# The last output block in two column halves, and new ranks in a list planner (gated linear recurrence followed by a SiLU MLP)

## The chip, the cores and the metric

One core of a Trainium2 chip. Times are device microseconds of one execution; the metric is the median of several runs. A profile is one execution, recorded by the hardware profiler; its span runs from the first to the last instruction.

## The reference

A recurrence with a forget gate over 768 positions, for 4 batches and 8 heads of 48 channels, and then an MLP with SiLU over the 3072 rows that come out of it:

```python
f = 1 / (1 + exp(-f_logit))                      # q, k, v, f_logit: [4, 8, 768, 48]
for t in range(768):
    state = f[:, :, t, :, None] * state + einsum('bhd,bhe->bhde', k[:, :, t], v[:, :, t])
    y[:, :, t] = einsum('bhd,bhde->bhe', q[:, :, t], state)
x = y.transpose(0, 2, 1, 3).reshape(3072, 384)   # heads side by side
h = x @ w_in                                     # w_in: [384, 2048]
out = (h * (1 / (1 + exp(-h)))) @ w_out          # w_out: [2048, 384]
```

## The kernel before

The work is cut into 12 blocks m, each with two units j. A unit is 128 positions of one batch, all heads: a block holds 256 rows of x. Block m belongs to chunk m // 2 of the sequence, so units of block m need the state that block m - 2 left (`st`).

A unit's recurrence is done in chunk form. `logs` takes ln(1 + exp(-f)) on ScalarE (task L), `cumsum` sums it along positions on TensorE (cs), `inverse` and `forward` take exponentials of it (ia, aa), `scale_k` on GpSimd and `scale_q` on VectorE multiply k and q by them (ki, qg). TensorE transposes both (T), VectorE copies the result out (qk), TensorE makes the scores (A), VectorE masks them (am), TensorE makes the outputs from scores and state (Y), VectorE copies them (yc), TensorE turns them so that channels stand on partitions (X), and VectorE copies that into `xT`. `update` (D) and `state` (st) carry the state on. Block 0 is laid out in another way (WIDE), which the change does not touch.

The MLP of a block: `mlp_in` (tasks I) makes h transposed, with w_in as weights, in 8 groups of six matmuls that stream 256 columns (both units) into one PSUM tile `h_ps`, and `silu` (S) writes it to `hT` in bf16. For blocks listed in SPLIT, `mlp_in_unit` and `silu_unit` do one unit at a time: twelve matmuls of 128 columns a group, again 8 groups a block. `mlp_out` (O) multiplies hT of a unit by w_out into `o_ps`, in four groups of four matmuls of 384 columns; `result` (R) copies it on ScalarE to `o_sb`, and `store` (G) sends 128 rows of 384 floats to the output, from GpSimd's queue for blocks under 8 and from SyncE's (SP) from block 8 (LATE) on. `h_ps`, `o_ps` and the fillers share three PSUM buffers.

The weights come in eight DMAs from GpSimd (`load_w_in` and `load_w_out`, 512 columns or 4 row tiles each), which are held back until ki of block 1, unit 1 has been done (BEFORE). The inputs come through SP's queue, into eight rotating buffers for each of f, k, q and v.

The order of everything is made at build time by the class `Plan`. Each task has an engine, a cost in us written in the code, the tasks that it needs, the buffers that it takes and frees, and a rank. `Plan.run` walks through time: of the tasks that could start first on an engine it takes the one with the lowest rank. The ranks are base = 8m + 3j (W["m"], W["j"]) plus an offset for each kind (W), and 1000 and more for the MLP, which so fills what the recurrence leaves. A TensorE task of block 3 or later is planned to start at least `spare` after the producer on another engine is done, over and above a fixed allowance (DRAIN). `patience` says how long the planner stays in one of the modes "MLP in" and "MLP out" on TensorE, since ScalarE has to load a table (`act_table`) when it turns from exponentials to SiLU. Where TensorE would wait for more than `slack`, the planner puts in filler matmuls on zeros (`warm`). The instructions are then written out in the order of the planned starts; each engine executes its own in that order, and waits by semaphores. So the planned times set the order and nothing else.

The groups of the views, by line: 489 narrow MLP-in matmuls, 504 wide ones, 519 MLP out, 524 the copy of the result, 530 its store, 535 fillers, 330 qg, 327 ki, 386 scores, 441 turns, 497 and 513 SiLU.

Of the kernel before, what the change touches and what calls it, by code (L numbers as in the profile page):

```python
# [11 lines left out]
F32 = mybir.dt.float32  # L12
# [6 lines left out]
class Plan:  # L19
# [58 lines left out]
    def run(self, filler=None):  # L78
# [5 lines left out]
        holder = {}  # L84
        left = dict(tasks)
        for t in tasks.values():
            for n in t["needs"]:
                assert n in tasks, (t["name"], n)
        self.silus = self.ins = self.exps = turned = 0
        while left:  # L90
            best = None
            fronts = {}
            for t in left.values():
                ready = 0.0
                for n in t["needs"]:
                    if n not in end:
                        ready = None
                        break
                    ready = max(ready, end[n] + (self.DRAIN.get(tasks[n]["engine"], 0.1) + t["spare"]) * (tasks[n]["engine"] != t["engine"]))
                if ready is None:  # L100
                    continue
# [24 lines left out]
            if e in ("LD", "WT"):  # L126
# [5 lines left out]
                if t["emit"] is not None:  # L132
                    self.order.append((start, t["emit"]))
                del left[t["name"]]
                continue
# [32 lines left out]
            self.log.append((start, end[t["name"]], e, t["name"]))  # L168
            del left[t["name"]]
        self.span = max(end.values())  # L170
# [17 lines left out]

    patience = 0.7
    slack = 0.4  # L190
    spare = 0.8

# [6 lines left out]
def kernel(  # L199
# [10 lines left out]
    nc = tc.nc  # L210
# [303 lines left out]

    def mlp_out(m, j, n):
        if n == 0:
            os[m, j] = hps.tile([C, d_model], F32, name="o_ps", tag="h_ps")
        for i in range(n, n + 4):
            nc.tensor.matmul(os[m, j], hT[m][:, i, j * C:(j + 1) * C], w_out_sb[:, i, :],  # L519
                             start=(i == 0), stop=(i == NT - 1))  # L520

    def result(m, j):
        osb[m, j] = wk.tile([C, d_model], F32, name="o_sb", bufs=4)
        nc.scalar.copy(osb[m, j], os[m, j])  # L524

    def store(m, j):
# [38 lines left out]
    for m in range(NH):  # L565
# [56 lines left out]
        for j in range(HB):  # L622
            for n in range(0, NT, 4):
                add(f"O{m}.{j}.{n}", "PE", 0.655, do(mlp_out, m, j, n),
                    [f"S{m}.{j}.{n}" if m in SPLIT else f"S{m}.{n + 2}", f"wo{n}"] + ([f"O{m}.{j}.{n - 4}"] if n else []),
                    rank=1000 + m * 10 + 5 + j + n * 0.1, takes="h" if n == 0 else None,
                    frees=[owner] if n == NT - 4 and j == HB - 1 else None)
            add(f"R{m}.{j}", "ACT", 0.5, do(result, m, j), [f"O{m}.{j}.{NT - 4}"], rank=-500.0, frees=[f"O{m}.{j}.0"])
            add(f"G{m}.{j}", *(("SP", 0.05) if m >= LATE else ("POOL", 0.85)), do(store, m, j), [f"R{m}.{j}"], rank=-501.0)
            add(f"W{m}.{j}", "DMA", 0.6, None, [f"G{m}.{j}"], rank=-1)  # L630

# [70 lines left out]
```

## Time and profile before

| | |
|---|---|
| runs, us | 195.43, 194.62, 194.53, 196.70, 195.81; median 195.43 |
| the profiled execution | 195.43 us, its span 193.7 us |
| granted TensorE clock | 1.00 |
| busy: TensorE, weight loads, VectorE, ScalarE, GpSimd | 96%, 73%, 58%, 67%, 29% |
| matmuls: MLP out, MLP in wide, MLP in narrow, fillers | 384, 432, 288, 75 of 2127 |
| table loads on ScalarE | 14, 1283 ns each |

The page counts a matmul from its issue to the end of its way through the array, so that matmuls overlap: what a group costs TensorE is the distance of starts and not the mean duration. In the lines shown further on, an entry such as "PE h_ps L504 x6" is TensorE, the tile written, the line and the number of matmuls; in the chain the two numbers ahead of it are start and length in us. A bracket at the end of a timeline row is the idle time of the engine ahead of it and what ended it. PEld is TensorE's weight load. In a row of groups, the part after the last bar is the idle time ahead of the group and what released it.

### The profile page before, as it was taken

What the parts mean: (1) busy time and instruction counts of PE and PEld (TensorE: products, weight loads), DVE (VectorE), ACT (ScalarE), POOL (GpSimd) and SP (SyncE); (2) the same over time, 40 slices, a digit from 0 to 9 for tenths busy, and PEclk for the clock granted to TensorE, in tenths of its full rate; (3) what the DMA queues carried; (4) which work ended last, traced back from release to release, by engine and by line L of the source; (5) the groups of instructions that cost most, each with busy time, mean ns of one, the idle gap of its engine ahead of it and who ended that gap; (6) DMA issues with size and microseconds to landing.
All of it is one profiled execution on the core that took longest, in us unless ns stands there. A gap on an engine that the chain in (4) does not pass through costs nothing.

```text
span 193.7 us, 5153 instructions
## 1 busy us (share of the span) xinstructions
PE 185.9 (96%) x2127; PEld 141.0 (73%) x2127; DVE 113.0 (58%) x222; ACT 130.5 (67%) x244; POOL 56.9 (29%) x84
## 2 busy tenths in 40 slices
PE   7789988999999999999999999999999999999993
PEld 3457767999666687878688688976688679886661
DVE  6188866652059993877379989726887883000000
ACT  2754556768876569898989995799775027993111
POOL 7343990010375423341571332007820000000000
PEclk9999999999999999999999999999999999999999
DMA  5999999998999999999999996001120020000222
GB/s 126 220 213 174 190 194 190 185 186 168 214 240 252 213 218 196 229 219 211 223 238 216 181 238 148 3 0 41 44 81 3 0 85 0 0 3 0 81 81 81
DMA packets 101654, 27.06 MB, mean 140 GB/s; under 512 B 96256, under 2 KB 100864, under 8 KB 101632
## 3 DMA queue, kind: packets, MB, share of 16 engines
q1 hardware_dynamic: 94784, 19.67, 52.0%
q0 software_dynamic: 4736, 6.29, 14.4%
q10 hardware_dynamic: 2112, 0.79, 2.2%
q8 instruction: 16, 0.26, 0.5%
q14 instruction: 6, 0.05, 0.1%
HBM read 25.17 MB, written 4.72 MB: 154 GB/s over the span
## 4 chain that ended last, share of the span: by engine, by line
PE 80%; DMA 9%; DVE 3%; POOL 3%; issue 2%; ACT 1%; ACTq 0%; DVEq 0%; POOLq 0%
PE o_ps L519 31%; PE h_ps L504 23%; PE h_ps L489 8%; DMA w_in_sb<-in_moe_w_in_dram 6%; PE t_ps L363 5%; DMA q_w<-in_q_dram 3%; PE a_ps L386 3%; PE y_ps L420 2%; PE y_ps L416 2%; PE x_ps L441 2%; PE cs L314 2%; PE d_ps L460 1%; DVE qg L330 1%; POOL ki L327 1%; PE al_ps L351 1%
## 5 line engine op out<-in xcount | busy, mean ns | idle before, releaser
L519 PE MATMUL o_ps<-w_out_sb,hT 128*128 128x384 bf16 x384 | 68.6, 326 | 0.0
L504 PE MATMUL h_ps<-xT,w_in_sb 128*128 128x256 bf16 x432 | 52.1, 273 | 0.9 <-DMA w_in_sb<-in_moe_w_in_dram 0.9
L519 PEld LDWEIGHTS <-hT 128*128 128x128 bf16 x384 | 36.2, 98 | 21.3
L513 ACT ACTIVATE hT<-h_ps 128x512 bf16<-128x512 f32 x72 | 42.4, 597 | 12.3 <-PE h_ps L504 9.8
L504 PEld LDWEIGHTS <-w_in_sb 128*128 128x128 bf16 x432 | 40.5, 98 | 6.4 <-DMA w_in_sb<-in_moe_w_in_dram 1.4
L327 POOL TENSOR_TENSOR ki<-k_ld,ia 128x384 bf16<-128x384 f32 x22 | 22.3, 1018 | 29.6 <-ACT ia L319 22.5
L330 DVE TENSOR_TENSOR qg<-q_ld,a 128x384 bf16<-128x384 f32 x22 | 19.8, 905 | 19.2 <-ACT a L324 19.0
L397 DVE TENSOR_TENSOR atm<-a_ps,triu 128x512 bf16<-128x512 f32 x44 | 28.3, 686 | 3.9 <-PE a_ps L386 3.8
L524 ACT COPY o_sb<-o_ps 128x384 f32<-128x384 f32 x24 | 11.5, 478 | 26.2 <-PE o_ps L519 26.0
L336 POOL CAST vb<-v_ld 128x384 bf16<-128x384 f32 x22 | 12.5, 567 | 40.1 <-DMA v_ld<-in_v_dram 34.9
L368 DVE COPY qk<-t_ps 128x1024 bf16<-128x1024 bf16 x24 | 16.4, 685 | 4.8 <-PE t_ps L363 4.7
L287 ACT ACT_TABLE_LOAD x14 | 18.0, 1283 | 1.8 <-PEq L686 1.6
L489 PE MATMUL h_ps<-xT,w_in_sb 128*128 128x128 bf16 x288 | 18.5, 219 | 0.0
L435 DVE CAST y<-y_ps 128x384 bf16<-128x384 f32 x22 | 12.2, 554 | 10.0 <-PE y_ps L420 9.9
L489 PEld LDWEIGHTS <-w_in_sb 128*128 128x128 bf16 x288 | 16.6, 98 | 0.6
L535 PE MATMUL w_ps<-zeros 128*128 128x384 bf16 x75 | 15.6, 351 | 1.2 <-DVE zeros L643 1.2
L497 ACT ACTIVATE hT<-h_ps 128x512 bf16<-128x512 f32 x24 | 13.9, 597 | 3.9 <-PE h_ps L489 3.1
L319 ACT ACTIVATE ia<-cs 128x384 f32<-128x384 f32 x24 | 11.4, 485 | 4.8 <-PE cs L314 4.1
L530 POOL DMA_DIRECT2D out_dram<-o_sb x16 | 9.3, 584 | 11.6 <-ACT o_sb L524 7.5
L301 ACT ACTIVATE f_ld<-f_ld 128x384 f32<-128x384 f32 x22 | 11.6, 526 | 1.5 <-DMA f_ld<-in_f_logit_dram 1.4
L480 DVE TENSOR_TENSOR states<-sd,al 48x192 bf16<-48x192 f32 x32 | 11.8, 368 | 0.8
L302 ACT ACTIVATE lf<-f_ld 128x384 bf16<-128x384 f32 x22 | 11.5, 523 | 0.7
(76 smaller groups left out, 198.3 us busy)
## 6 DMA issues: line engine op xcount, KB each, us to landing
f_ld<-in_f_logit_dram SPq DMA_DIRECT2D x22, 192.0 KB, 4.1
k_ld<-in_k_dram SPq DMA_DIRECT2D x22, 192.0 KB, 4.3
q_ld<-in_q_dram SPq DMA_DIRECT2D x22, 192.0 KB, 4.2
v_ld<-in_v_dram SPq DMA_DIRECT2D x22, 192.0 KB, 4.1
out_dram<-o_sb POOLq DMA_DIRECT2D x16, 192.0 KB, 3.5
w_in_sb<-in_moe_w_in_dram POOLq DMA_DIRECT2D x4, 384.0 KB, 9.6
w_out_sb<-in_moe_w_out_dram POOLq DMA_DIRECT2D x4, 384.0 KB, 17.5
out_dram<-o_sb SPq DMA_DIRECT2D x8, 192.0 KB, 1.9
```

The lines of the kernel that those rows point to most:

```text
L287: nc.scalar.preload_act_table_set(tables[name])
L327: nc.gpsimd.tensor_mul(slots(m, ki[m % 4][:, j, :, 0:D]), flip(m, loaded[m, j, "k"]), slots(m, ias[m, j]))
L330: nc.vector.tensor_mul(slots(m, qg[m % 4][:, j, :, 0:D]), flip(m, loaded[m, j, "q"]), slots(m, aas[m, j]))
L336: nc.gpsimd.tensor_copy(vb[m % 4][:, j], loaded[m, j, "v"])
L368: nc.vector.tensor_copy(qkT[m, j], t_ps[m, j])
L397: nc.vector.tensor_mul(atm[m, j][:, r], att[m, j][:, r], triu[:, None, :].to_broadcast([C, NP, C]))
L489: nc.tensor.matmul(h_ps[:, i], w_in_sb[:, kk, (n + i) * 128:(n + i + 1) * 128], xT[m][:, kk, j], start=(kk == 0), stop=(kk == KT - 1))
L497: nc.scalar.activation(hT[m][:, n:n + 4, j * C:(j + 1) * C], hs[m, j, n], AF.Silu)
L504: nc.tensor.matmul(h_ps[:, i], w_in_sb[:, kk, (n + i) * 128:(n + i + 1) * 128], xT[m][:, kk].rearrange("p b c -> p (b c)"), start=(kk == 0 ...
L513: nc.scalar.activation(hT[m][:, n:n + 2, :], hs[m, n], AF.Silu)
L519: nc.tensor.matmul(os[m, j], hT[m][:, i, j * C:(j + 1) * C], w_out_sb[:, i, :], start=(i == 0), stop=(i == NT - 1))
L535: nc.tensor.matmul(w_ps[:, 0:NP * 2 * D], zeros[:, 0:128], zeros, start=True, stop=True)
```

## The change

Three things, in one diff.

The last unit's MLP-out (block 11, unit 1) is made in two column halves of 192, each with its own PSUM tile, its own four groups, its own copy and its own store; the second half's groups come after the first's. All other units keep 384 columns.

The numbers that the planner goes by are other ones: all ranks in W except that of m, SPLIT (blocks 1, 2, 3 before, 2 alone after), `patience` (0.7 to 0.5), `spare` (0.8 to 0.5), and the block from which `spare` holds (3 to 5). The cost of a result's copy is 0.05 higher.

The planner's bookkeeping: it keeps a list of the tasks whose needs are done, with their ready times, and breaks ties of rank by the order in which tasks were added, as they stood in its table before.

```diff
-        spare = self.spare if engine == "PE" and m >= 3 else 0.0
+        spare = self.spare if engine == "PE" and m >= self.spare_from else 0.0
...
-            for t in left.values():
-                ready = 0.0
-                for n in t["needs"]:
...
+            for t in could.values():
+                if t["name"] not in ready_at:
+                    ready_at[t["name"]] = max([0.0] + [
...
-                choice = min(now, key=lambda c: c[2]["rank"])
+                choice = min(now, key=lambda c: (c[2]["rank"], place[c[2]["name"]]))
...
-    patience = 0.7
+    patience = 0.5
     slack = 0.4
-    spare = 0.8
+    spare = 0.5
+    spare_from = 5
...
-    def mlp_out(m, j, n):
+    def mlp_out(m, j, n, cols):
         if n == 0:
-            os[m, j] = hps.tile([C, d_model], F32, name="o_ps", tag="h_ps")
+            os[m, j, cols] = hps.tile([C, d_model], F32, name="o_ps", tag="h_ps")
+        lo, hi = cols
         for i in range(n, n + 4):
-            nc.tensor.matmul(os[m, j], hT[m][:, i, j * C:(j + 1) * C], w_out_sb[:, i, :],
+            nc.tensor.matmul(os[m, j, cols][:, lo:hi], hT[m][:, i, j * C:(j + 1) * C], w_out_sb[:, i, lo:hi],
                              start=(i == 0), stop=(i == NT - 1))
...
-    def result(m, j):
-        osb[m, j] = wk.tile([C, d_model], F32, name="o_sb", bufs=4)
-        nc.scalar.copy(osb[m, j], os[m, j])
+    def result(m, j, cols):
+        lo, hi = cols
+        osb[m, j, cols] = wk.tile([C, d_model], F32, name="o_sb", bufs=4)
+        nc.scalar.copy(osb[m, j, cols][:, lo:hi], os[m, j, cols][:, lo:hi])
...
-        eng.dma_start(out=out[r0:r0 + C, :], in_=osb[m, j])
+        eng.dma_start(out=out[r0:r0 + C, lo:hi], in_=osb[m, j, cols][:, lo:hi])
...
-    W = dict(m=8, j=3, L=0, cs=0, ia=-15, aa=1, ki=4, qg=1, vb=-8, T=7, qk=1, A=7, am=-2, Y=11,
-             yc=1, D=25, st=-3, X=4, xT=-9, al=-4, ea=3, va=13)
+    W = dict(m=8, j=6, L=-8, cs=1, ia=-11, aa=-5, ki=1, qg=3, vb=-13, T=28, qk=10, A=3, am=10, Y=15,
+             yc=6, D=12, st=-4, X=-27, xT=-18, al=-28, ea=-4, va=36)
     LATE = 8
-    SPLIT = (1, 2, 3)
+    SPLIT = (2,)
...
+            parts = [(0, d_model)] if (m, j) != (NH - 1, HB - 1) else [(0, d_model // 2), (d_model // 2, d_model)]
+            for part, cols in enumerate(parts):
+                part = "abc"[part]
+                share = (cols[1] - cols[0]) / d_model
+                for n in range(0, NT, 4):
+                    add(f"O{m}.{j}.{n}{part}", "PE", 0.655 * share, do(mlp_out, m, j, n, cols),
...
+                        rank=1000 + m * 10 + 5 + j + n * 0.1 + 2 * (part == "b"), takes="h" if n == 0 else None,
...
+                add(f"R{m}.{j}{part}", "ACT", 0.5 * share + 0.05, do(result, m, j, cols), [f"O{m}.{j}.{NT - 4}{part}"],
+                    rank=-500.0, frees=[f"O{m}.{j}.0{part}"])
+                add(f"G{m}.{j}{part}", *(("SP", 0.05) if m >= LATE else ("POOL", 0.85)), do(store, m, j, cols),
+                    [f"R{m}.{j}{part}"], rank=-501.0)
```

More of the change, by code (lines that the diff above doesn't have):

```diff
@@ L85, in run, with done @@
         left = dict(tasks)
+        place, users, missing, ready_at = {}, {}, {}, {}
         for t in tasks.values():
-            for n in t["needs"]:
+            place[t["name"]] = len(place)
+            missing[t["name"]] = len(set(t["needs"]))
+            for n in set(t["needs"]):
                 assert n in tasks, (t["name"], n)
+                users.setdefault(n, []).append(t["name"])
+        could = {n: t for n, t in tasks.items() if not missing[n]}
+        def done(name):
+            for u in users.get(name, ()):
+                missing[u] -= 1
+                if not missing[u]:
+                    could[u] = tasks[u]
+            del left[name], could[name]
         self.silus = self.ins = self.exps = turned = 0
@@ L92, in run @@
             fronts = {}
-            for t in left.values():
-                ready = 0.0
[L95 to L101, printed above, removed]
+            for t in could.values():
+                if t["name"] not in ready_at:
+                    ready_at[t["name"]] = max([0.0] + [
+                        end[n] + (self.DRAIN.get(tasks[n]["engine"], 0.1) + t["spare"]) * (tasks[n]["engine"] != t["engine"])
+                        for n in t["needs"]])
+                ready = ready_at[t["name"]]
                 p = self.pool_ready(t, end)
@@ L133, in run @@
                     self.order.append((start, t["emit"]))
-                del left[t["name"]]
+                done(t["name"])
                 continue
@@ L168, in run @@
             self.log.append((start, end[t["name"]], e, t["name"]))
-            del left[t["name"]]
+            done(t["name"])
         self.span = max(end.values())
@@ L513, in silu, with store @@
         nc.scalar.activation(hT[m][:, n:n + 2, :], hs[m, n], AF.Silu)
-    def mlp_out(m, j, n):
+    def mlp_out(m, j, n, cols):
         if n == 0:
-            os[m, j] = hps.tile([C, d_model], F32, name="o_ps", tag="h_ps")
+            os[m, j, cols] = hps.tile([C, d_model], F32, name="o_ps", tag="h_ps")
+        lo, hi = cols
         for i in range(n, n + 4):
-            nc.tensor.matmul(os[m, j], hT[m][:, i, j * C:(j + 1) * C], w_out_sb[:, i, :],
+            nc.tensor.matmul(os[m, j, cols][:, lo:hi], hT[m][:, i, j * C:(j + 1) * C], w_out_sb[:, i, lo:hi],
                              start=(i == 0), stop=(i == NT - 1))
-    def result(m, j):
-        osb[m, j] = wk.tile([C, d_model], F32, name="o_sb", bufs=4)
-        nc.scalar.copy(osb[m, j], os[m, j])
-    def store(m, j):
+    def result(m, j, cols):
+        lo, hi = cols
+        osb[m, j, cols] = wk.tile([C, d_model], F32, name="o_sb", bufs=4)
+        nc.scalar.copy(osb[m, j, cols][:, lo:hi], os[m, j, cols][:, lo:hi])
+    def store(m, j, cols):
+        lo, hi = cols
         g, b = m // 2, m % 2 * HB + j
@@ L622 @@
         for j in range(HB):
[L623 to L630, printed above, removed]
+            parts = [(0, d_model)] if (m, j) != (NH - 1, HB - 1) else [(0, d_model // 2), (d_model // 2, d_model)]
[4 more added lines that the diff above has]
+                    add(f"O{m}.{j}.{n}{part}", "PE", 0.655 * share, do(mlp_out, m, j, n, cols),
+                        [f"S{m}.{j}.{n}" if m in SPLIT else f"S{m}.{n + 2}", f"wo{n}"]
+                        + ([f"O{m}.{j}.{n - 4}{part}"] if n else []),
+                        rank=1000 + m * 10 + 5 + j + n * 0.1 + 2 * (part == "b"), takes="h" if n == 0 else None,
+                        frees=[owner] if n == NT - 4 and j == HB - 1 and cols == parts[-1] else None)
+                add(f"R{m}.{j}{part}", "ACT", 0.5 * share + 0.05, do(result, m, j, cols), [f"O{m}.{j}.{NT - 4}{part}"],
+                    rank=-500.0, frees=[f"O{m}.{j}.0{part}"])
+                add(f"G{m}.{j}{part}", *(("SP", 0.05) if m >= LATE else ("POOL", 0.85)), do(store, m, j, cols),
+                    [f"R{m}.{j}{part}"], rank=-501.0)
+                add(f"W{m}.{j}{part}", "DMA", 0.6 * share, None, [f"G{m}.{j}{part}"], rank=-1)
     pieces = [("wi", load_w_in, n) for n in range(0, d_ff, 512)] + [("wo", load_w_out, n) for n in range(0, NT, 4)]
```

## The prediction

> **What bounds the kernel now.** I read the busy shares first, then the slices, then the chain that ended last, then TensorE's own pieces of it, and last the end of the span. The first view gives shares only:
>
> ```profile
> PE 185.9 (96%) x2127; PEld 141.0 (73%) x2127; DVE 113.0 (58%) x222; ACT 130.5 (67%) x244; POOL 56.9 (29%) x84
> ...
> PE   7789988999999999999999999999999999999993
> ...
> DMA  5999999998999999999999996001120020000222
> ...
> PE 80%; DMA 9%; DVE 3%; POOL 3%; issue 2%; ACT 1%; ACTq 0%; DVEq 0%; POOLq 0%
> ```
>
> The slices say more than the share: from about the sixth to the last PE stands at 9, so the time is the sum of PE's work from its first MLP group to its last, plus the few holes in it, plus the tail. The reader is to see that a moved instruction on DVE, ACT or POOL is worth nothing unless PE waits for it.
>
> The holes show in the timeline of PE about 33 us and in the chain about 62 to 67 us. The columns are start and duration in us.
>
> ```profile
> 31.72 0.83 PE L489 MATMUL h_ps<-xT,w_in_sb 128*128 128x128 bf16 x12
> 33.05 0.83 PE L504 MATMUL h_ps<-xT,w_in_sb 128*128 128x256 bf16 x6 [0.50 <-DMA w_in_sb<-in_moe_w_in_dram]
> ```
> ```profile
> 62.13 1.39 DVE qg L330
> 63.52 0.48 DVE sd L477
> ...
> 64.75 0.56 DVE y L435
> ...
> 65.34 1.30 DVE atm L397 x2
> ...
> 66.68 0.40 PE a_ps L386 x8
> ```
>
> The first pair: twelve narrow matmuls take 0.67 us, so PE was free at 32.39 and stood 0.66 us for a piece of w_in. The second: DVE is the chain for 4.5 us (62.13 to 66.64); PE had ended its transposes x_ps (start 66.16, 0.17 long) at 66.33, a score group starts about 0.10 late after any other kind of group (62.07 after an o_ps group that began at 61.32 and issues for 0.65), so 0.25 us of the 0.35 is a true wait. I find no third hole over 0.1 us after 27 us, except one filler matmul w_ps at 75.9 (0.16 us), which is a hole that the plan filled. So after 27.0 us PE has only 0.66 + 0.25 + 0.16 = 1.07 us that isn't work.
>
> The unit costs of PE, and the end:
>
> ```profile
> 34.42 0.66 PE h_ps L504 x6
> ...
> 35.25 0.67 PE h_ps L489 x12
> ```
> ```profile
> L524 ACT COPY o_sb<-o_ps 128x384 f32<-128x384 f32 x24 | 11.5, 478 | 26.2 <-PE o_ps L519 26.0
> ...
> out_dram<-o_sb SPq DMA_DIRECT2D x8, 192.0 KB, 1.9
> ```
> ```profile
> 190.45 0.48 ACT L524 COPY o_sb<-o_ps 128x384 f32<-128x384 f32 x1 [1.47 <-PE o_ps L519]
> ```
>
> The last matmul ends at 190.37, the copy runs to 190.93, the store is issued at 190.96 and lands 1.9 us later, and the closing semaphores bring the span to 193.7. The tail after PE is 3.3 us.
>
> **What the Trainium skill says.** "TensorE: Matmul & The Clock Gate", section "Back-to-back issue gap", gives N/2.4 + 2.5 ns for one matmul of N columns, and a slower 81 ns for N=128 where a weight load goes with each. The trace agrees with the first (0.67/12 = 56 ns at 128, 0.655/6 = 109 ns at 256, 0.65/4 = 163 ns at 384) and not with the 81. "ScalarE: Activation LUTs", section "What ACT_TABLE_LOAD costs", has a fixed part of 186 ns and 0.833 ns per column, and 1283 ns for a table load; the trace has 478 ns for 384 columns, somewhat under, and 1283 ns for the load. "DMA: Bandwidth & Descriptors", section "Latency and other measured facts", puts the fixed cost of a transfer near 2 us, mostly the round trip; the 1.9 us of these stores agrees, so half the bytes cannot halve it. "GPSIMD Engine Reference", section "1. Specifications", says that GpSimd shares its SBUF interfaces with VectorE when the latter has two SBUF inputs. qg is such an operation: 0.54 us at its shortest, 1.39 us at 62.13 while POOL's ki ran from 62.10.
>
> **The change part by part.**
>
> *The narrow groups (SPLIT).* Blocks 1 and 3 go from 16 narrow groups of twelve 128-column matmuls to 16 wide ones of six with 256: 96 matmuls fewer, but 16 x (0.670 - 0.655) = 0.24 us less PE time, no more, since columns set the pace and not instructions. Their Silus stay 16 of 597 ns. What it adds is a wait: a wide group of a block needs both transposed halves (xT), a narrow one only its own. For block 1 this comes at 32 us, where in the trace both xT copies are done by 31; and the next thing there, the third piece of w_in at 33.05, is a DMA whose queue order is unchanged. So the 0.66 us hole stays, and the work ahead of it is the same. For block 3 the first wide group waits for the second half's xT; in the order of the changed kernel it stands behind the output groups of block 2, so its cost goes with the stalls below.
>
> *The filler.* The program has 85 matmuls fewer: 96 narrow ones off, 16 on for the last result, so 5 fillers off. The order has none after the first MLP group, so the one at 75.9 goes: 0.16 us. The other four stood before 27 us, where w_in ends the wait: nothing.
>
> *The last result in halves.* 16 matmuls of 384 columns become 32 of 192. Same columns: the formula gives 82.5 ns, and the wide cumulative sums (192 columns at 7.97 and 8.05) show 80; 32 x 0.08 = 2.6 us against 16 x 0.163 = 2.6 us. Nothing, at worst 32 x 0.018 = 0.6 us if each weight load of 98 ns had to be sat out, which the 56 ns spacing of the narrow groups speaks against. The first half is copied and stored while PE does the second half's 1.3 us, so its copy, its issue on SP (0.33 us) and its transfer are covered. After the last matmul stand a copy of 192 columns and a store of 96 KB. The copy: the exp on 8 columns takes 181 ns and the copy on 384 takes 478, so 0.79 ns a column, about 0.33 us for 192: 0.15 us saved. The store: 0.2 us saved, an estimate between 0 (all round trip) and 0.35 (half of 0.66 us, the part of the last store in which its packets run, 191.79 to 192.45). Together 0.35 us, bounds 0.1 to 0.5, less by up to 0.6 in the bad case of the loads.
>
> *Ranks and spare.* The order is new on all engines from the start. Up to the weights' issue POOL and SP stand as before, so PE's first MLP group stays at 27.0 us. ACT gets two table loads more (16 for 14), 2.6 us; ACT is busy 67%, waits 26 us for o_ps and 9.8 us for h_ps, and PE has output groups queued at these places: nothing, at most 2.6. The wait at 66.68 goes with its neighbours' order: -0.25. What comes instead decides. Before, PE's due times kept 0.8 us of spare behind each producer from block 3 on; now 0.5 us from block 5 on and none for blocks 3 and 4. In the new order about ten PE groups of these two blocks (T, A, X, Y between 55 and 78 us) stand right behind the copy or product that feeds them, where before none did. What can make a producer late is seen in the chain above: the plan gives qg 1.0, state 1.12, y 0.55, atm 1.32, in all 3.99 us, and DVE took 4.51; 0.5 us late, and PE waited 0.25 us although it had 0.8 us of spare. A wait once taken shifts everything behind it, so the same lateness isn't paid ten times. I take 0.5 us for the stage. From block 5 on, 0.5 us of spare should hold nearly everything; included. Bounds: 0 (over a whole block the plan's DVE costs, 5.07 us, equal the measured 0.905 + 0.685 + 1.37 + 0.554 + 1.29 + 0.354 = 5.16), and ten times 0.4 = 4.0 us if each is caught by a new overlap of qg with ki. Behind a waiting PE group stand all later ones, in strict order; ACT's Silus and the stores follow them.
>
> *Sum.* -0.24 - 0.16 - 0.35 - 0.25 + 0.5 = -0.5 us against the profiled execution of 195.43 us (span 193.7 and 1.7 around it), which is also the median of the runs. Forecast 194.9 us. The bookkeeping in the planner (ready lists, ties by place) changes no cost.
>
> **Rivals.**
> *No new stall.* For it: the DVE costs add up over a block, and between 27 and 50 us PE runs as tightly behind its producers with no wait but the weights'. Against: the 4.51 us chain. Then -1.0, 194.4 us; with the tail at its best and 0.4 us more from holes under 0.1 us, 193.9.
> *Nothing gained at the end.* The store's time is all round trip and the stalls take 0.8 us: -0.24 - 0.16 - 0.15 - 0.25 + 0.8 = 0, 195.4 us. For it: 1.9 us to landing for 192 KB as for the smallest transfers; against: 0.66 us of packets are there to be seen.
> *Slower: blocks 3 and 4 without spare.* One mechanism: DVE's qg runs beside POOL's ki at 1.4 instead of 0.55 to 1.0 us, each time just ahead of a copy on which PE's next group stands. Price 0.4 us a place; ten places give 4.0 us in place of 0.5: 198.4 us. It decides over 1% from eight places on (2.95 us of stalls against the 1.0 us of gains). For it: every number in it is in the trace; against: a shift by one stall leaves the next producers early.
> The change does what it says: both halves stand at the end of PE's order.
>
> **How the numbers follow.** A difference of 1%, about 2 us, is what a measurement of this kernel can tell from no change; the five runs spread over 2.2 us. Forecast 0.45, no stall 0.23 (a third of it past 1% with favours that I can't name), nothing gained 0.17, slower rival 0.15, nearly all of it past 1%. That gives faster 0.08, same 0.78, slower 0.14. The range takes in the no-stall rival's best and leaves out most of the slower one: 193.5 to 197.0.
>
> **What would show it.** Right: first MLP group still at 27.0 us and the hole before 33.05 still there; the narrow groups down from 288 to 96 matmuls and the wide ones up from 432 to 528; no filler after 30 us; one or two holes of 0.2 to 0.5 us on PE between 55 and 80 us ended by DVE; last copy 0.33 us; tail after the last matmul about 3.0 us. Wrong: PE's holes between 50 and 84 us over 1.5 us in sum, DVE or ACT as the chain there for more than 5 us, the second-half matmuls over 90 ns apart, or a new wait for w_in or f_ld.

## The result, and the profile after

The changed kernel takes 196.64 us (median of 43 runs, 195.51 to 198.4) against 195.12 us of the kernel before (80 runs, 194.33 to 197.33). The ratio is 1.0076, with an interval of 1.0061 to 1.0091: 1.5 us slower where 0.5 us faster was forecast. The profiled execution took 196.57 us with a span of 194.9; before it was 195.43 and 193.7. So 1.14 us of the difference lie in the span and can be looked for in the trace. A ratio here leaves out executions more than 1.5% above the fastest one of the same kernel, so it need not be the quotient of the medians.

The shares and the slices of the profile page show where not to look:

```profile
PE 186.4 (96%) x2042; PEld 140.4 (72%) x2042; DVE 114.6 (59%) x222; ACT 132.7 (68%) x247; POOL 57.5 (29%) x84
...
PE   7999988999999999999999999999999999999993
...
PE 83%; DMA 4%; DVE 3%; issue 3%; ACT 2%; POOL 2%; ACTq 0%; POOLq 0%
...
L515 PE MATMUL h_ps<-xT,w_in_sb 128*128 128x256 bf16 x528 | 63.8, 273 | 1.2 <-DMA w_in_sb<-in_moe_w_in_dram 1.2
```

PE is still at 9 in almost every slice, and the 528 wide matmuls are the number that the prediction gave. A loss of 1 us in 195 doesn't show in shares; it has to be looked for in PE's timeline, hole by hole, and after PE's last matmul. There are four places.

**About 30 us.** PE's timeline there (start, duration, what, in brackets the idle time before it and what ended it):

```profile
27.73 0.82 PE L515 MATMUL h_ps<-xT,w_in_sb 128*128 128x256 bf16 x6
...
28.98 0.39 PE L374 MATMUL t_ps<-ident,ki 128*128 128x128 bf16 x4
30.06 0.83 PE L515 MATMUL h_ps<-xT,w_in_sb 128*128 128x256 bf16 x6 [0.69 <-DMA w_in_sb<-in_moe_w_in_dram]
...
31.98 2.14 PE L515 MATMUL h_ps<-xT,w_in_sb 128*128 128x256 bf16 x18
```

Four transposes from 28.98 are issued by 29.21, so PE stands for 0.85 us until the second piece of w_in is there. In the kernel before, a narrow group of block 1 stood in this gap, from 29.14 to 29.81:

```profile
29.14 0.83 PE L489 MATMUL h_ps<-xT,w_in_sb 128*128 128x128 bf16 x12
```

The old hole of 0.66 us ahead of the third piece is gone: the 18 matmuls from 31.98 run through. At the eighth MLP group, the first wide one that stands behind the same work in both kernels (34.49 after, 34.26 before), this execution is 0.23 us behind, 0.07 of it from a first MLP group at 27.07 instead of 27.00. That isn't the price of the new order: the same mark lies at 33.81 to 34.55 us in the five traces of the old order (the kernel before and four of the runs below), and at 33.91 to 34.59 in six further traces of the new one. It shifts with the arrival of the weights.

**About 58 us.** The timeline of all engines, a few rows of it:

```profile
54.70 2.92 POOL L338 TENSOR_TENSOR ki<-k_ld,ia 128x384 bf16<-128x384 f32 x3
55.60 2.51 DVE L341 TENSOR_TENSOR qg<-q_ld,a 128x384 bf16<-128x384 f32 x1 [2.13 <-ACT a L335]
...
56.52 1.46 PE L531 MATMUL o_ps<-w_out_sb,hT 128*128 128x384 bf16 x8
...
58.04 0.68 DVE L379 COPY qk<-t_ps 128x1024 bf16<-128x1024 bf16 x1
58.64 0.54 DVE L341 TENSOR_TENSOR qg<-q_ld,a 128x384 bf16<-128x384 f32 x1
58.77 0.40 PE L397 MATMUL a_ps<-qk 48*128 48x128 bf16 x8 [0.78 <-DVE qk L379]
```

Read it from the bottom. The scores of block 3's first unit (a_ps, 58.77) wait for the copy qk. That copy's input had been there since 56.7, but on DVE it stands behind qg of the next unit, and this qg took 2.51 us where the next one takes 0.54. Beside it POOL runs three ki without a pause, 54.70 to 57.62. Eight output matmuls of 0.163 us occupy PE from 56.52 to 57.82; less the 0.10 us by which a score group comes late behind other groups in these traces, PE lost 0.85 us.

**About 87 us.** The chain that ended last (start, duration, what):

```profile
84.34 0.21 PE d_ps L471 x4
...
84.58 0.57 DVE sd L488
...
85.17 0.68 DVE states L491
...
85.86 0.72 DVE states L491
...
86.61 0.70 DVE qk L379
...
87.36 0.61 PE t_ps L374 x8
```

The transposes of block 6 (t_ps, 87.36) need the one t_ps buffer. It is freed by the copy qk of block 5's second unit, which stands on DVE behind that block's state work. 18 wide matmuls of 0.109 us from 84.82 occupy PE until 86.79, so PE lost 0.57 us. (The 0.10 us is not taken off here: it stands ahead of score groups alone, and the other transposes behind MLP-in groups in this trace start with no gap. Where an expectation below says 0.47 us, read 0.57.) The two state multiplications took 1.40 us; of one alone the trace has 0.35.

**The end.** The last copies in the timeline, the rows of SP's stores among the DMA issues (KB each, median us from issue to landing), and SP's closing wait:

```profile
190.22 0.32 ACT L537 COPY o_sb<-o_ps 128x192 f32<-128x192 f32 x1 [0.51 <-PE o_ps L531]
191.54 0.32 ACT L537 COPY o_sb<-o_ps 128x192 f32<-128x192 f32 x1 [1.00 <-PE o_ps L531]
```
```profile
out_dram<-o_sb SPq DMA_DIRECT2D x7, 192.0 KB, 1.9
...
out_dram<-o_sb SPq DMA_DIRECT2D x2, 96.0 KB, 1.6
```
```profile
SPq L719 <- DMA out_dram<-o_sb: 1.2, 1, 1.2
```

The copy of 192 columns takes 0.32 us for 0.48, and its store lands after 1.6 us for 1.9. From the last matmul's end (191.455) to the end of SP's wait for that landing are 2.09 us, before 2.47 (190.37 to 192.84): 0.38 us saved. But the span ends 3.40 us after the last matmul, before 3.34. What lies between is a list of semaphore waits with which SP closes the program. These are the ends of its entries in us, from the records of SP's sequencer; "landing" marks the entry that has the last store's semaphore:

```
before:  191.36  191.43  191.50  191.56  191.62  191.68  191.74  191.80  192.84 landing          span ends 193.71
after:   192.29  193.55 landing  193.61  193.68  193.74  193.80  193.86  193.92  193.98          span ends 194.85
```

Nine entries in both, each 0.06 us when its semaphore is there already, in a fixed order. Before, the last store was awaited last, and everything else had been asked while it flew. After, it is awaited second, and seven entries of 0.06 us stand behind it: 0.43 us. Why second: SP's stores take their semaphores in rotation out of eight; with the last result in halves SP issues nine stores of results instead of eight, so the last one gets the semaphore that the first had.

In sum: unsplit groups -0.24, filler -0.16, the wait at 66.68 us -0.25, landing -0.38; against it +0.85, +0.57, +0.23 and the list +0.43. That makes +1.05 of the 1.14 us in the span.

### The profile page after: what moved, and what is told of

It is laid out like the page before. It is cut to its first block, busy times and chain, and to the rows that moved or that the text cites. A ratio compares the mean times of both kernels' runs of the same rounds, so it can differ in the third digit from the quotient of the medians.

```text
span 194.9 us, 4983 instructions
## 1 busy us (share of the span) xinstructions
PE 186.4 (96%) x2042; PEld 140.4 (72%) x2042; DVE 114.6 (59%) x222; ACT 132.7 (68%) x247; POOL 57.5 (29%) x84
## 4 chain that ended last, share of the span: by engine, by line
PE 83%; DMA 4%; DVE 3%; issue 3%; ACT 2%; POOL 2%; ACTq 0%; POOLq 0%
PE o_ps L531 30%; PE h_ps L515 28%; PE t_ps L374 5%; DMA w_in_sb<-in_moe_w_in_dram 4%; PE a_ps L397 3%; PE w_ps L549 3%; PE h_ps L500 3%; PE y_ps L431 2%; PE x_ps L452 2%; PE y_ps L427 2%; PE d_ps L471 2%; PE cs L325 1%; DVE qg L341 1%; DVE qk L379 1%; POOL ki L338 1%
## 5 line engine op out<-in xcount | busy, mean ns | idle before, releaser
L531 PE MATMUL o_ps<-w_out_sb,hT 128*128 128x384 bf16 (+1 forms) x400 | 69.1, 319 | 0.0
L524 ACT ACTIVATE hT<-h_ps 128x512 bf16<-128x512 f32 x88 | 51.5, 597 | 20.8 <-PE h_ps L515 18.0
L515 PE MATMUL h_ps<-xT,w_in_sb 128*128 128x256 bf16 x528 | 63.8, 273 | 1.2 <-DMA w_in_sb<-in_moe_w_in_dram 1.2
L515 PEld LDWEIGHTS <-w_in_sb 128*128 128x128 bf16 x528 | 49.6, 98 | 7.6 <-DMA w_in_sb<-in_moe_w_in_dram 1.6
L531 PEld LDWEIGHTS <-hT 128*128 128x128 bf16 x400 | 37.4, 98 | 20.8
L338 POOL TENSOR_TENSOR ki<-k_ld,ia 128x384 bf16<-128x384 f32 x22 | 23.3, 1072 | 46.9 <-ACT ia L330 46.2
L537 ACT COPY o_sb<-o_ps 128x384 f32<-128x384 f32 (+1 forms) x25 | 11.6, 465 | 22.0 <-PE o_ps L531 21.8
L335 ACT ACTIVATE a<-cs 128x384 f32<-128x384 f32 x24 | 11.9, 496 | 0.0
L549 PEld LDWEIGHTS <-zeros 128*128 128x128 bf16 x70 | 7.4, 111 | 6.2 <-issue 2.9
L457 DVE COPY xT<-x_ps 128x384 bf16<-128x384 bf16 x24 | 8.5, 355 | 5.2 <-PE x_ps L452 4.8
```

The costliest lines, as they stand in the source:

```text
L338: nc.gpsimd.tensor_mul(slots(m, ki[m % 4][:, j, :, 0:D]), flip(m, loaded[m, j, "k"]), slots(m, ias[m, j]))
L515: nc.tensor.matmul(h_ps[:, i], w_in_sb[:, kk, (n + i) * 128:(n + i + 1) * 128], xT[m][:, kk].rearrange("p b c -> p (b c)"), start=(kk == 0 ...
L524: nc.scalar.activation(hT[m][:, n:n + 2, :], hs[m, n], AF.Silu)
L531: nc.tensor.matmul(os[m, j, cols][:, lo:hi], hT[m][:, i, j * C:(j + 1) * C], w_out_sb[:, i, lo:hi], start=(i == 0), stop=(i == NT - 1))
L549: nc.tensor.matmul(w_ps[:, 0:NP * 2 * D], zeros[:, 0:128], zeros, start=True, stop=True)
```

## The experiments

The theory after this reading: the new order costs 0.85 and 0.57 us because of two places in DVE's order, and the halves gain nothing because of the list. The rivals: the loss is spread over many tight places in blocks 3 and 4; or half-width matmuls and stores cost by themselves. Each ratio is to the kernel before on the same chip, where its median was 195.11, 195.40 or 195.52 us.

### The two parts apart

*The last result in halves in the old order* (`halves_alone`; ranks, SPLIT, patience and spare as before; the copy's cost without the 0.05, so that the order stays):

```diff
-    patience = 0.5
-    spare = 0.5
-    spare_from = 5
+    patience = 0.7
+    spare = 0.8
+    spare_from = 3
...
-    SPLIT = (2,)
+    SPLIT = (1, 2, 3)
```

> The last result in two halves, with the ranks, spare, patience, SPLIT and the order of all other instructions of the kernel before. Theory 'closing list' (the halves' copy and store save 0.4 us, but the ninth store on SP takes the semaphore that SP's closing list asks for second instead of last, and seven more entries of 0.065 us follow its landing): the tail after the last matmul stays at 3.3 to 3.4 us and the time at that of before, 0.0 to +0.1 us. Rival 'halves gain' (the prediction's 0.35 us): -0.35 us. Rival 'halves cost' (two half groups slow TensorE): last groups over 90 ns a matmul and +0.3 us or more.

Measured: 195.97 us, ratio 1.0027 (1.0005 to 1.0048). The halves alone do not gain; they lose a little at most. In its trace the tail is 3.40 us (last matmul 190.61, landing awaited until 192.71, list until 193.14, span 194.0), the same as in the changed kernel. Its span is 0.3 us longer than before; 0.06 of that is the tail, the rest the arrival of the weights (eighth MLP group at 34.55 us for 34.26).

*The new order with the last result whole* (`ranks_alone`):

```diff
-            parts = [(0, d_model)] if (m, j) != (NH - 1, HB - 1) else [(0, d_model // 2), (d_model // 2, d_model)]
+            parts = [(0, d_model)]
```

> The changed kernel with its last result in one piece: ranks, spare, patience and SPLIT alone. Theory 'three holes' (the time went into TensorE waits at 30, 58.8 and 87.4 us that the new order brings): +1.1 us over before in the span, the three holes at 0.84, 0.85 and 0.5 us as in the changed kernel, 196.3 to 196.7 us. Rival (the halves are what costs): within 0.3 us of before.

Measured: 196.87 us, ratio 1.0065 (1.004 to 1.0091). PE stands before the same three groups, 0.82 us at 29.5, 1.30 at 58.6 (with the usual 0.10) and 0.56 at 87.1, and its tail is 3.35 us. The hole at 58.6 is larger than in the changed kernel: qg took 2.58 us there. So nearly all of the loss belongs to the order, not to the halves.

### Where the last store stands in SP's list

Both kernels with halves again (`halves_lane` in the old order, `after_lane` in the new), with one store of block 8's first unit moved from SP to POOL's queue, so that SP issues eight and the last store gets the last semaphore:

```diff
-        eng = nc.sync if m >= LATE else nc.gpsimd
+        eng = nc.sync if m >= LATE and (m, j) != (8, 0) else nc.gpsimd
```

> As halves_alone, but the store of block 8, unit 0 goes by GpSimd's queue, so that SP issues eight stores and the last one has the semaphore that the closing list asks for last. Nothing else moves. Theory 'closing list': tail 2.9 to 3.0 us, 0.4 us under before and under halves_alone, 194.7 us where before has 195.1. Rival (the list is of no account, or the half store's landing is all round trip): as halves_alone within 0.1 us.

Measured: 195.39 us, ratio 0.9998 (0.9969 to 1.0027). The tail falls from 3.40 to 2.94 us (last matmul 189.96, landing awaited until 192.04 as the last entry, span 192.9). The last copy in the chain that ended last, first with the landing second in the list, then with it last:

```profile
187.98 2.65 PE o_ps L531 x30
...
190.69 0.32 ACT o_sb L537
```
```profile
187.98 1.99 PE o_ps L531 x24
...
190.04 0.32 ACT o_sb L537
```
```profile
core 0: 194.0 us, clock 0.999
```
```profile
core 0: 192.9 us, clock 1.000
```

From the start of this copy to the end of the span are 3.3 us in the first and 2.9 in the second. The halves and the last store are the same, so it is not the half-width transfer that was slow. The median doesn't resolve the gain: 0.2% under the kernel before was expected, and the interval holds both that and nothing.

> The changed kernel with the store of block 8, unit 0 on GpSimd's queue; nothing else moves. Theory 'closing list': tail 2.9 to 3.0 us for 3.4, so 0.45 us under the changed kernel: 196.2 us, +0.55% over before. Rival: as the changed kernel, +0.76%.

Measured: 196.91 us, ratio 1.008 (1.0049 to 1.0111, 12 runs). Its trace shows the short tail, 2.96 us (190.79 to 193.74), but the median does not show the gain. This is a miss: it should have been about 0.2% faster than the changed kernel (1.0076) and than the new order with the last result whole (1.0065), and came out 0.04% and 0.15% slower, inside the intervals.

The converse (`list_shifted`) leaves the kernel before as it is, whole result and old order, and only gives SP a ninth store by issuing one early store as two:

```diff
-        eng.dma_start(out=out[r0:r0 + C, :], in_=osb[m, j])
+        for lo in (0, d_model // 2) if (m, j) == (8, 0) else (0,):
+            hi = lo + d_model // 2 if (m, j) == (8, 0) else d_model
+            eng.dma_start(out=out[r0:r0 + C, lo:hi], in_=osb[m, j][:, lo:hi])
```

> The kernel before, with the store of block 8, unit 0 issued as two DMAs of 192 columns, 35 us ahead of the end; the last result, its copy and its store are whole as before. SP then issues nine stores, and the last one has the semaphore that the closing list asks for second. Theory 'closing list': the tail after the last matmul grows from 3.35 to 3.8 us, +0.45 us, 0.2% over before, with nothing changed in the last 30 us but the place in the list. Rival (the list is of no account): tail 3.35 us and the time of before within 0.1 us.

Measured: 196.06 us, ratio 1.0053 (1.0029 to 1.0078). The tail grows from 3.34 to 3.79 us (last matmul 190.905, landing awaited until 193.39 as the second entry, list until 193.83). The chain's last piece and the span:

```profile
190.99 0.48 ACT o_sb L524
```
```profile
core 0: 194.7 us, clock 1.000
```

Nothing about the last result differs from the kernel before. So the place in the list is enough to cost 0.45 us of tail. The median says more than that: 0.45 us are 0.23%, which lies below the interval. Its trace has waits of PE of 0.39 us at 66.7 and 0.54 at 72.4, well ahead of the first store on SP at 155.5, so they have nothing to do with the list; what else raised the median is open. The tails agree: second in the list 3.40, 3.40 and 3.79 us (halves, halves, whole); last in it 2.94, 2.96, and 3.34 and 3.35 us (halves, halves; whole, whole). The later runs with halves repeat it: 3.39 to 3.40 us where the landing is second, 2.95 where it is last.

### The two places in DVE's order

*Block 3* (`qk30_first`). In the changed kernel, qg of block 3's second unit is written out behind the copy qk of its first, instead of ahead of it; the other queues keep their order. In `Plan.emit`:

```diff
+    moves = [('qg3.1', 'qk3.0')]
...
+        for what, behind in self.moves:
+            at = [n for n, _ in todo].index(what)
+            it = todo.pop(at)
+            todo.insert([n for n, _ in todo].index(behind) + 1, it)
```

> The changed kernel with one instruction moved: VectorE makes qg of block 3, unit 1 after the copy qk of unit 0 and not ahead of it. Theory 'three holes': the wait of TensorE at 58.8 us (0.85 us past the usual 0.10) goes, since the copy no longer stands behind a product that ran 2.51 us beside GpSimd's three ki; -0.85 us against the changed kernel, +0.3% over before; the hole at 87 us stays. Rival (TensorE would have waited anyway, for the transposes or the next score group): the wait moves by under 2 us and the time stays within 0.2 us of the changed kernel's.

Measured: 196.31 us, ratio 1.0017 (0.9992 to 1.0043). The timeline where the hole was:

```profile
54.36 2.92 POOL L346 TENSOR_TENSOR ki<-k_ld,ia 128x384 bf16<-128x384 f32 x3
...
56.39 0.69 DVE L387 COPY qk<-t_ps 128x1024 bf16<-128x1024 bf16 x1 [3.25 <-PE t_ps L382]
...
57.00 1.61 DVE L349 TENSOR_TENSOR qg<-q_ld,a 128x384 bf16<-128x384 f32 x2
...
57.59 0.40 PE L405 MATMUL a_ps<-qk 48*128 48x128 bf16 x8
...
58.20 0.40 PE L382 MATMUL t_ps<-ident,qg 128*128 128x128 bf16 x4 [0.21 <-DVE qg L349]
```

POOL's three ki are still there. The copy now goes ahead at 56.39, the scores follow the output group at once, and what is late next is the transposes of the delayed qg, 0.28 us. The hole at 86.5 us stays (0.58). One moved instruction takes 0.6% off the ratio. In this trace a wait of 0.34 us for the third piece of w_in is back at 32.95.

*Both* (`qk_both_first`). The state work of block 5's first unit is written out behind qk of its second as well:

```diff
-    moves = [('qg3.1', 'qk3.0')]
+    moves = [('qg3.1', 'qk3.0'), ('st5.0', 'qk5.1')]
```

> As qk30_first, and the state of block 5, unit 0 made after the copy qk of unit 1. Theory 'three holes': the hole at 87 us (0.47 us past the usual) goes too, -1.3 us against the changed kernel, +0.1% over before; what stays is w_in's hole near 30 us and the tail. Rival: the state comes late for its reader, or the wait moves on; no more than 0.2 us below qk30_first.

Measured: 196.03 us, ratio 1.0013 (0.9994 to 1.0033); its span is 193.6 us.

```profile
84.37 0.69 DVE L387 COPY qk<-t_ps 128x1024 bf16<-128x1024 bf16 x1 [1.03 <-PE t_ps L382]
84.98 0.55 DVE L496 TENSOR_TENSOR sd<-d_ps,states 128x384 f32<-128x384 f32 x1
85.56 0.74 DVE L499 TENSOR_TENSOR states<-sd,al 48x192 bf16<-48x192 f32 x2
...
86.14 0.39 PE L382 MATMUL t_ps<-ident,qg 128*128 128x128 bf16 x4
```

The second hole is gone too; the transposes no longer wait, and both state multiplications together take 0.74 us, where they had taken 1.40; of POOL's work only the last 0.15 us of a cast stand beside the first of them. Left on PE are 0.75 us at 29.7, 0.29 at 58.2 and two of 0.11 to 0.14 near 71.5. In the span the second move is worth 0.4 us (194.0 to 193.6); in the ratio its share (0.04%) is less than the intervals can tell.

*The same hole from the other engine* (`ki40_later`). To see that it is POOL's ki, not the length of DVE's queue, DVE is left as changed, and POOL writes out the third ki behind the cast vb of its unit, so that two ki run side by side with qg and not three:

```diff
+    moves = [('ki4.0', 'vb4.0')]
```

> The changed kernel with one instruction moved on GpSimd: ki of block 4, unit 0 after the cast vb of that unit, so that two ki in place of three stand beside VectorE's qg at 55.6 us. Theory 'qg stands still while ki runs' (alone 0.55 us, 2.51 us beside 2.12 us of ki): qg takes 1.5 to 1.9 us, the wait at 58.8 us falls to 0.3 us or less, -0.6 us or more against the changed kernel. Rival (qg's length comes from the data's arrival or from the exponentials, not from GpSimd): qg 2.5 us and the wait as they were.

Measured: 196.29 us, ratio 1.0037 (1.0012 to 1.0063).

```profile
54.33 1.97 POOL L346 TENSOR_TENSOR ki<-k_ld,ia 128x384 bf16<-128x384 f32 x2
...
55.23 1.50 DVE L349 TENSOR_TENSOR qg<-q_ld,a 128x384 bf16<-128x384 f32 x1 [1.64 <-ACT a L343]
...
56.65 0.68 DVE L387 COPY qk<-t_ps 128x1024 bf16<-128x1024 bf16 x1
...
57.25 0.54 DVE L349 TENSOR_TENSOR qg<-q_ld,a 128x384 bf16<-128x384 f32 x1
57.26 1.39 POOL L346 TENSOR_TENSOR ki<-k_ld,ia 128x384 bf16<-128x384 f32 x1
57.55 0.40 PE L405 MATMUL a_ps<-qk 48*128 48x128 bf16 x8
```

qg in the same place takes 1.50 us instead of 2.51, for one ki less beside it, and the hole is gone though nothing moved on DVE. The late ki makes a new wait of 0.43 us at 65.1, and the hole at 86.6 stays (0.57). So the 0.85 us need two things at once, qg ahead of the copy on DVE and three ki in a row beside it on POOL; taking away either one removes the hole.

The last two lines of POOL and DVE show one thing more. The second qg began 0.01 us ahead of the third ki, and here it is ki that is slowed: qg takes 0.54 us, ki 1.39 in place of 1.0.

### Is it the unsplit groups?

The changed kernel with blocks 1 and 2 in narrow groups (`split12`), in case both the wait for w_in and what follows come from SPLIT:

```diff
-    SPLIT = (2,)
+    SPLIT = (1, 2)
```

> The changed kernel with block 1 in narrow groups again (SPLIT 1 and 2), order planned anew. Theory 'three holes': the narrow group of block 1 stands ahead of the first group that needs w_in's second piece, so the hole at 30 us shrinks from 0.7 to 0.85 us to under 0.2, and one of 0.4 to 0.7 us comes back ahead of the third piece, as before: at most 0.2 us won; the hole near 58 us stays at 0.8 us or more, since qg and the three ki stand as in the changed kernel. Rival: the hole near 58 us is a matter of the MLP groups' width, and goes.

One execution: 197.9 us. A narrow group stands in the gap at 29.0 again and the wait of 0.85 us there is gone. There are other holes: 1.36 us at 36.1, where a qg is late that had itself waited for its input q_ld, and the one in block 3:

```profile
55.50 2.91 POOL L338 TENSOR_TENSOR ki<-k_ld,ia 128x384 bf16<-128x384 f32 x3
...
56.41 2.86 DVE L341 TENSOR_TENSOR qg<-q_ld,a 128x384 bf16<-128x384 f32 x1 [2.13 <-ACT a L335]
...
59.92 0.40 PE L397 MATMUL a_ps<-qk 48*128 48x128 bf16 x8 [1.14 <-DVE qk L379]
```

With block 1 in narrow groups, three ki stand beside a qg of 2.86 us again. So the hole in block 3 doesn't come from block 1's groups but from the ranks and the spare, which no run separates. A single time of this kernel says little on the whole, and the late q_ld isn't shown to come from SPLIT: the next kernel, with SPLIT as changed, has the like.

### Everything mended, and the old order with the same means

*The changed kernel with both moves and the store moved to POOL's queue* (`mended`):

```diff
+    moves = [('qg3.1', 'qk3.0'), ('st5.0', 'qk5.1')]
...
-        eng = nc.sync if m >= LATE else nc.gpsimd
+        eng = nc.sync if m >= LATE and (m, j) != (8, 0) else nc.gpsimd
```

> qk_both_first, with the store of block 8, unit 0 on GpSimd's queue. Both theories together: holes at 58.8 and 87 us gone, tail 2.95 us; -1.75 us against the changed kernel, 194.9 us or 0.1 to 0.2% under before. If the time is at or over before's by more than its interval, a cost is missing in the account.

Measured: 195.46 us, ratio 0.9994 (0.9964 to 1.0024). That is the time of the kernel before; the 0.1 to 0.2% under it that was expected can't be told from nothing. Its profiled execution, 197.95 us, lay 2.5 us above its own median. Both holes are gone in it and the tail is 2.95 us, but PE waits 1.17 us at 39.2 for a qg whose q_ld came late and 0.91 at 44.3 for a cast whose v_ld came late. Late inputs of this kind make part of the spread of the times.

*The kernel before with halves, the moved store, and its own wait at 66.7 us taken away* (`best`), by writing the two state multiplications of block 3's first unit behind the masked scores of its second:

```diff
+    held = {}
...
+            held[3, 1] = scale
...
+        if (m, j) in held:
+            held.pop((m, j))()
```

> The order of the kernel before, the last result in halves, the store of block 8, unit 0 on GpSimd's queue, and the two multiplications of the state of block 3, unit 0 made after the masked scores of unit 1 (its sum stays where it was). Expected from the account: tail 2.95 for 3.34 us (-0.4), and the wait of TensorE at 66.7 us (0.25 past the usual) gone: -0.65 us, 0.3% under before. Rival (the halves cost TensorE or the waits move on): at before's time.

Measured: 195.71 us, ratio 0.9988 (0.9957 to 1.0018); the medians of all executions, 195.71 and 195.11, point the other way. The wait is gone, the scores follow right behind the transposes:

```profile
67.12 0.33 PE L455 MATMUL x_ps<-ident,y 128*128 128x128 bf16 x3
...
67.39 0.40 PE L398 MATMUL a_ps<-qk 48*128 48x128 bf16 x8
```

Expected gains of 0.25 us at this wait and 0.4 us at the tail are 0.3% together; the interval holds both that and nothing. The rival that the waits move on has something for it: this trace has waits of 0.21 to 0.61 us at 42.2, 58.8, 61.3 and 65.4. And the wait at 66.7 isn't a fixed cost of the old order: it is 0.25 us in the kernel before and 0.39 in `list_shifted`, but the two other traces with the old order untouched, `halves_alone` and `halves_lane`, have none. No version measured here is shown to beat the kernel before.

**What returns in every trace.** A wait in one trace may be chance, so here the traces are laid side by side, from the eighth MLP group to PE's last matmul. Without its waits of over 0.1 us, PE takes 155.85 to 155.91 us there in the five traces of the old order and 155.50 to 155.55 in the seven of the new one (the SPLIT variant apart): the unsplit groups and the missing filler are worth their 0.3 to 0.4 us each time. The hole near 58 us stands in all three traces of the new order in which neither of the two moves against it was made (0.85, 1.21 and 0.77 us past the usual, in the changed kernel, with the last result whole, with the moved store), and the one near 87 us in all five without the second move (0.56 to 0.58). No trace of the old order has a wait of over 0.3 us at either place. For the two profiled executions the parts now add up: weights +0.23, PE's own work -0.31, the waits +1.42 for 0.26, the tail +0.06, in all the 1.14 us of the span.

## Why the prediction was wrong, point by point

- **The narrow groups, -0.24 us; the filler, -0.16.** As worked out: 528 wide matmuls, no filler after 25.3 us, and 0.3 to 0.4 us less work on PE in every trace.
- **The wait at 66.68, -0.25: right for one execution only.** It is gone, but two of the four traces with that part of the old order untouched don't have it. The term was read off a single profile.
- **"The 0.66 us hole stays, and the work ahead of it is the same": failed as a reading, with no cost shown.** The hole of 0.66 us gave way to one of 0.85 us ahead of the second piece. The working looked only at the copies (xT) that a wide group of block 1 needs, and at the third piece of w_in. The narrow groups' place mattered: one of them had filled the gap ahead of the second piece. This is the "new wait for w_in" that the prediction named as a sign against it. In sum the weights cost about the same in both orders, as the marks of the eighth MLP group say; the 0.66 us itself is 0.55 in `halves_alone` and absent in three other traces of the old order.
- **"I take 0.5 us for the stage": the term that failed.** The two stalls that DVE ends took 0.85 and 0.57 us, 1.4 in sum; with both moved away the ratio falls from 1.0076 to 1.0013. The first is in the stage that the prediction named, blocks 3 and 4, and takes 0.77 to 1.21 us there in place of 0.5; its cause is the one named in the slower rival, qg beside ki. The price of 0.4 us a place was read from a qg beside one ki (1.39 us). Whether several ki stand in a row was not asked, though the order of the changed kernel tells it. So the rival's mechanism held, with one place of 0.85 us instead of ten of 0.4.
- **"From block 5 on, 0.5 us of spare should hold nearly everything": failed, by 0.57 us.** The prediction put this stage at nothing. In `Plan.run`, `spare` is added to the end of the tasks in `needs`; the time at which a buffer comes free (`pool_ready`) has none. The transposes of block 6 waited for a buffer, so by the code 0.8 us of spare would have added nothing at this place either.
- **The last result in halves, -0.35 us: right in its parts, and then lost.** Copy and landing gave 0.38 us (copy 0.32 instead of 0.33 us, packets of the last store 0.44 instead of 0.68). The Trainium skill, "DMA: Bandwidth & Descriptors", section "Latency and other measured facts", puts the fixed cost of a transfer near 2 us. The trace agrees that most of the time doesn't follow the bytes, half of which took 1.6 us for 1.9; the whole is somewhat under the page's figure. The step that failed is the end of the sum: the prediction let "the closing semaphores" follow the landing at an unchanged price. With a ninth store, seven more entries of the list follow it, +0.43 us. "A tail of about 3.0 us" was measured as 3.40; with the last store at the end of the list it is 2.94.
- **Second-half matmuls at the formula's 82.5 ns, table loads at nothing.** Right: the 192-column matmuls are 0.08 us apart, and none of the holes is ended by a table load.
- **The range.** The measured 196.64 us lies inside 193.5 to 197.0, but with the sign reversed: a loss of 1.5 us where a gain of 0.5 was forecast. That is luck of a wide range, not the working.
- **The rivals.** "Nothing gained at the end" has the right outcome for the tail with the wrong reason: the landing did come earlier. "No new stall" is refuted by the moves. The slower rival's 198.4 us was too much, since in blocks 3 and 4 only one place lost time, the one beside three ki; the second stall lies outside its stage.

What stays open. The medians differ by 0.4 us more than the two profiled spans. In the medians the list's effect points the expected way in three pairs (halves -0.3%, mended -0.2%, list shifted +0.5%) and not in the fourth (+0.15%); the first two are within their intervals and the third is more than twice what the list explains, so its size there is less sure than the 0.45 us in the tails. No run changes the spare alone, so it isn't shown whether 0.8 us of it in blocks 3 and 4 would have hidden the first stall. What slowed the first of the two state multiplications at 85.17 us, when POOL issued a DMA and then only began its cast at 85.84, is not shown; it takes 0.67 to 0.68 us in the same place in five more traces.

## What to carry to other kernels

When a planner's order changes, ask at each place without spare not only what a producer costs but what runs on the neighbouring engine in the same microseconds, and how many such instructions stand in a row; and check whether the margin in the plan also covers waits for buffers. Before a last transfer is cut in two, look at what follows its landing: here a half microsecond of closing waits was hidden behind the landing, and one store more on that queue brought it out. Two instructions moved on the DVE queue gave back nearly all that a new order had cost, so repair the places before choosing another order. And before a wait is booked to an order, see whether it stands in a second trace of that order: the stalls near 58 and 87 us do, the waits for w_in and the one at 66.7 us come and go.

## What the runs showed of the hardware that I had not expected

- qg on DVE hardly moves on while POOL runs a ki that began before it. Alone it takes 0.54 to 0.56 us; beside one ki (1.0 us of overlap) 1.39 to 1.53; beside 2.0 us of three ki 2.51. The time added is nearly the overlap itself (2.51 - 0.55 = 1.96 for 2.02 us; an expectation's 2.12 counts the ends where two ki overlap twice). The Trainium skill, "GPSIMD Engine Reference", section "1. Specifications", says that the two engines share their SBUF interfaces when VectorE has two SBUF inputs; these are the prices of it here.
- Where qg began ahead of a ki, ki could be the one slowed (0.54 and 1.39 us in `ki40_later` at 57.25). A shift of 0.2 us can turn this round: the same qg of the old order began 0.03 us behind a ki in the kernel before and took 1.39 us, with PE's wait at 66.68 us after it, and began 0.19 us ahead of it in `halves_alone` and took 0.64, with no such wait.
- Beside POOL's issuing of a DMA alone qg takes 0.54 to 0.55 us. Where the issue was still running as qg began and a cast or a ki followed it, both outcomes occur: 0.56 us in the changed kernel at 52.92 but 1.05 in `ki40_later` at 52.55, with the same cast 0.1 us behind, and 1.92 beside an issue and a ki in the kernel before at 132.55. What decides there is open.
- A state multiplication takes 0.35 us alone and 0.65 to 0.72 us beside a cast of POOL of about 0.5 us that began just ahead of it.
- The closing list on SP costs about 0.06 us for each entry behind the last landing, 0.43 us for seven.
